# Pooled attention and a maxout feed-forward layer on one core: two shared score and AV buffers, an overlapped last token chunk, and a gate on the second batch's loads

## The chip, the cores and the metric

The kernel runs on one core of one Trainium2 chip. The metric is device time in microseconds (us) of one execution; lower is better. The core has TensorE (PE, with its weight loads as PEld), VectorE (DVE), ScalarE (ACT), GpSimd (POOL) and SyncE (SP), each working through its own list of instructions in order, and 16 DMA engines that all queues share.

## What is computed

Inputs are q, k, v of shape (8 batches, 8 heads, 576 tokens, 64) in float32, three weights w1, w2, w3 (512 x 768) and w_out (768 x 512). Keys and values are averaged over groups of 8 tokens, so that each head has 72 pooled keys. The result is (4608, 512) in float32.

```python
k_p = k.reshape(B, H, Sp, pool, D).mean(axis=3)
v_p = v.reshape(B, H, Sp, pool, D).mean(axis=3)
scores = scale * np.matmul(q, k_p.transpose(0, 1, 3, 2))
attn = softmax(scores)                     # over the 72 pooled keys
attn_out = np.matmul(attn, v_p)
x = attn_out.transpose(0, 2, 1, 3).reshape(B * S, H * D)
h = np.maximum(np.maximum(x @ w1, x @ w2), x @ w3)
out = h @ w_out
```

## The kernel before

The work is staged by batch. `load` (L56) issues three loads of a batch: `kt` and `vt` (1.18 MB each) from SP's queue, and `qb` from POOL's queue, which turns float32 into bfloat16 on the way. Two buffers of each exist (pool `ld`). After the loads of batch 0, POOL builds two identity matrices and issues the loads of the three weights `mw` and of `mwo` on its queue (L79, L80).

`prep` (L93) folds the 8 tokens of each group by adding halves: three steps on `kt` into `kp2`, twice written (L98, L101), on DVE for batch 0 and on POOL for the others; and three steps on `vt` into `vp_all`, always on POOL. TensorE transposes `qb` in three groups of six into `pqt` (L114), ACT copies each group to `qT` (L116). TensorE transposes `kp2` into `pkt` (L120), and DVE spreads it into `kz` (L124), whose zeros let one matmul take even or odd tokens.

`heads` (L129) makes, for each of 8 heads, two matmuls into `psc` (L135) and one exponential on ACT, `et` (L138). `psc` takes two PSUM banks, and there is one `psc` buffer. `values` (L145) goes over the batch's 576 tokens in five chunks: four of 128 and one of 64, the short one last in even batches and first in odd ones. For each chunk it makes 8 matmuls into `pav` (L151; one buffer of two banks), a reciprocal and a product on DVE (`rcp` L157, `xn` L159), four transposes into `pxt` (L164) and a copy on ACT into `xT` (L168). `pqt`, `pkt` and `pxt` share a single bank, tag `tr`.

`moe` (L171) takes 512 tokens: 72 matmuls of 512 columns into `pw` (L179, three banks), the maxima on ACT and DVE (L184, L187, L190), then 24 matmuls into `po` (L196), a copy on ACT (`osb`, L200) and the stores of the output from SP (L204). There are nine such blocks; block n is emitted after `values(n+1)`, and the last two after batch 7.

The order on each engine is not the written order: a scheduler places the instructions of all stages, so that `moe(n)` is mixed with `prep`, `heads` and `values` of batch n+1. Each engine then takes its list strictly in order, and a buffer is given out again when its last reader has finished.

Of the kernel before, what the change touches and what calls it, by code (L numbers as in the profile page):

```python
# [10 lines left out]
ALU = mybir.AluOpType  # L11
# [3 lines left out]
def kernel(  # L15
# [11 lines left out]
    nc = tc.nc  # L27
    dt = mybir.dt
    F32, BF16, F16 = dt.float32, dt.bfloat16, dt.float16

    B, H, S, D = q.shape
    POOL = 8
    Sp = S // POOL
# [19 lines left out]
    etp = ctx.enter_context(tc.tile_pool(name="etp", bufs=16))  # L53
    psp = ctx.enter_context(tc.tile_pool(name="psp", bufs=1, space=PSUM))

    def load(b):  # L56
        kt = ld.tile([96, 6, POOL, D], F32, name="kt", tag="kt")
        nc.sync.dma_start(out=kt, in_=k[b].rearrange(  # L58
            "h s d -> (h s d)").rearrange("(p i j d) -> p i j d", p=96, i=6, j=POOL))
        vt = ld.tile([Sp, H, POOL, D], F32, name="vt", tag="vt")  # L60
        nc.sync.dma_start(out=vt, in_=v[b].rearrange(
            "h (sp j) d -> sp h j d", j=POOL))
        qb = ld.tile([128, 2, NT, D], BF16, name="qb", tag="qb")
        nc.gpsimd.dma_start(out=qb, in_=q[b].rearrange(  # L64
            "h s d -> (h s d)").rearrange("(g p t d) -> p g t d", g=2, p=128, t=NT))
        return kt, vt, qb

    first = load(0)

    ident = const.tile([128, 128], BF16, name="ident", tag="ident")  # L70
    make_identity(nc, ident)
    identh = const.tile([128, 128], F16, name="identh", tag="identh")
    make_identity(nc, identh)

    w_sb = [const.tile([128, KCH, DFF], F16, name=f"mw{wi}", tag=f"mw{wi}")
            for wi in range(3)]
    wo_sb = const.tile([128, JCH, C], F16, name="mwo", tag="mwo")
    for t, wap in zip(w_sb, (moe_w1, moe_w2, moe_w3)):
        nc.gpsimd.dma_start(out=t, in_=wap.rearrange("(kc p) j -> p kc j", p=128))  # L79
    nc.gpsimd.dma_start(out=wo_sb,  # L80
                        in_=moe_w_out.rearrange("(jc p) c -> p jc c", p=128))

    vp_all = const.tile([Sp, B, H, 65], F16, name="vp", tag="vp")
# [7 lines left out]
    xT = const.tile([128, KCH, TOK], F16, name="xT", tag="xT")  # L91

    def prep(b, kt, vt, qb):  # L93
        eng = nc.vector if b == 0 else nc.gpsimd
        kp2 = sb2.tile([96, 6, 2, D], BF16, name="kp2", tag="kp2")
        def fold(e, t, outs):
            for n in (4, 2):
                e.tensor_tensor(out=t[:, :, 0:n, :], in0=t[:, :, 0:n, :],  # L98
                                in1=t[:, :, n:2 * n, :], op=ALU.add)
            for o in outs:  # L100
                e.tensor_tensor(out=o, in0=t[:, :, 0, :], in1=t[:, :, 1, :],  # L101
                                op=ALU.add)

        fold(eng, kt, [kp2[:, :, 0, :], kp2[:, :, 1, :]])
        fold(nc.gpsimd, vt, [vp_all[:, b, :, 0:D]])

        qT = sb2.tile([128, 2, NI, 128], BF16, name="qT", tag="qT")
        qTf = qT.rearrange("p g i c -> p (g i) c")
        for m in range(3):
            pqt = psp.tile([128, 6, 128], BF16, name="pqt", tag="tr", bufs=1)  # L110
            for u in range(6):
                n = 6 * m + u
                g, i = n // NI, n % NI
                nc.tensor.transpose(pqt[:, u, :], qb[:, g, 2 * i:2 * i + 2, :],  # L114
                                    ident)
            nc.scalar.copy(out=qTf[:, 6 * m:6 * m + 6, :], in_=pqt)  # L116

        pkt = psp.tile([128, 6, 96], BF16, name="pkt", tag="tr", bufs=1)
        for i in range(6):
            nc.tensor.transpose(pkt[:, i, :], kp2[:, i, :, :], ident[0:96, 0:96])  # L120
        kz = kz_all[b % 2]
        for par in range(2):
            rows = slice(64 * par, 64 * par + 64)
            nc.vector.tensor_copy(  # L124
                out=kz[rows, par].rearrange("p h (r i) -> p h r i", i=6),
                in_=pkt[rows].rearrange("p i (h r) -> p h r i", h=H))
        return qT, kz

    def heads(b, qT, kz):  # L129
        ets = []  # L130
        for h in range(H):
            psc = psp.tile([Sp, 2, 512], F32, name="psc", tag="psc", bufs=1)
            mov = qT[:, h // 4, :, 32 * (h % 4):32 * (h % 4) + 32]
            for par in range(2):
                nc.tensor.matmul(psc[:, par, 0:288], kz[:, par, h, :], mov,  # L135
                                 start=True, stop=True)
            et = etp.tile([Sp, S], F16, name="et", tag="et")
            nc.scalar.activation(  # L138
                out=et.rearrange("p (i a r) -> p i a r", a=2, r=NR),
                in_=psc[:, :, 0:288].rearrange("p a (i r) -> p i a r", r=NR),  # L140
                func=FT.Exp, scale=1.0 / 64.0)
            ets.append(et)
        return ets

    def values(b, ets):  # L145
        c0 = 0
        for n in ((128, 128, 128, 128, 64) if b % 2 == 0
                  else (64, 128, 128, 128, 128)):
            pav = psp.tile([128, 2, 512], F32, name="pav", tag="pav", bufs=1)
            for h in range(H):  # L150
                nc.tensor.matmul(  # L151
                    pav[0:n, h // 4, 65 * (h % 4):65 * (h % 4) + 65],
                    ets[h][:, c0:c0 + n], vp_all[:, b, h, :],
                    start=True, stop=True)
            pv = pav[0:n, :, 0:260].rearrange("p g (h e) -> p g h e", e=65)
            rcp = sb3.tile([128, 2, 4], F32, name="rcp", tag="rcp")
            nc.vector.reciprocal(out=rcp[0:n], in_=pv[:, :, :, 64])  # L157
            xn = sb3.tile([128, 2, 4, D], F16, name="xn", tag="xn")
            nc.vector.tensor_tensor(  # L159
                out=xn[0:n], in0=pv[:, :, :, 0:D],  # L160
                in1=rcp[0:n].to_broadcast([n, 2, 4, D]), op=ALU.mult)
            pxt = psp.tile([128, KCH, 128], F16, name="pxt", tag="tr", bufs=1)
            for kc in range(KCH):
                nc.tensor.transpose(  # L164
                    pxt[:, kc, 0:n], xn[0:n, kc // 2, 2 * (kc % 2):2 * (kc % 2) + 2, :],
                    identh[0:n, 0:n])
            g0 = S * b + c0
            nc.scalar.copy(out=xT[:, :, g0:g0 + n], in_=pxt[:, :, 0:n])  # L168
            c0 += n

    def moe(n):  # L171
        col = slice(NB * n, NB * n + NB)
# [32 lines left out]

    done = 0
    for b in range(B):
        loaded = first if b == 0 else load(b)
        qT, kz = prep(b, *loaded)
        ets = heads(b, qT, kz)  # L210
        values(b, ets)
        while b >= 1 and (done + 1) * NB <= b * S:
            moe(done)
            done += 1
# [33 lines left out]
```

## Time and profile before

| | us |
|---|---|
| median of 3 runs | 305.67 |
| lowest and highest | 305.3 and 309.04 |
| the profiled execution, device time | 308.39 |
| its span, first to last instruction | 306.6 |
| its busy time on PE, ACT, DVE, POOL | 257.3, 133.0, 127.8, 124.6 |

The span is what the rows of the trace describe; 1.8 us of the profiled execution lie outside it. A row's first number is its start in us from the beginning of the span, where the view is one in order of time.

### The profile page before, as it was taken

To read this page: it belongs to the slowest core of one execution; us is meant where nothing else is said; L and a number is where in the kernel's file an instruction comes from. 1 tells how busy PE (TensorE), PEld (TensorE's weight loads), DVE (VectorE), ACT (ScalarE), POOL (GpSimd) and SP (SyncE) were. 2 spreads that over 40 slices of the span, in tenths; PEclk is the share of its full clock that TensorE was granted. 3 is DMA by queue.
4 is the path that set the end of the run, shared out by engine and by line. 5 is a ranking of instruction groups with operands and counts; after the bars stand their busy time and mean duration, and the time that the engine had idled before them with its cause. 6 is when DMAs were issued, how large, how long until landed. Compare 5 with 4: busy or idle time off the path is not lost.

```text
span 306.6 us, 4320 instructions
## 1 busy us (share of the span) xinstructions
PE 257.3 (84%) x1664; PEld 130.4 (43%) x1664; DVE 127.8 (42%) x211; ACT 133.0 (43%) x219; POOL 124.6 (41%) x72
## 2 busy tenths in 40 slices
PE   0144470299999999999999999999999999999991
PEld 0022330154455555445555544555554445444440
DVE  6410330043626563354537254625645262551530
ACT  1034220135476545545674654466546636214221
POOL 6059799749999997969600030000000000000000
PEclk9999996579999999999999999999999999999998
DMA  7999999988644986982610450050022003104014
GB/s 175 264 268 252 229 237 211 234 186 202 158 103 104 216 198 151 246 183 67 118 38 0 112 104 3 9 131 1 0 70 69 2 0 94 45 0 121 19 25 114
DMA packets 17078, 36.47 MB, mean 119 GB/s; under 512 B 2720, under 2 KB 5024, under 8 KB 16288
## 3 DMA queue, kind: packets, MB, share of 16 engines
q1 hardware_dynamic: 12512, 28.32, 35.7%
q0 software_dynamic: 4544, 7.87, 14.8%
q8 instruction: 13, 0.21, 0.3%
q14 instruction: 9, 0.07, 0.1%
HBM read 34.60 MB, written 9.44 MB: 144 GB/s over the span
## 4 chain that ended last, share of the span: by engine, by line
PE 78%; DMA 18%; POOL 1%; DVE 0%; ACT 0%; issue 0%; SPq 0%; ACTq 0%
PE pw L179 46%; PE po L196 15%; DMA qb<-in_q_dram 12%; DMA vt<-in_v_dram 6%; PE psc L135 5%; PE pav L151 4%; PE pqt L114 3%; PE pxt L164 3%; POOL vt L98 1%; PE pkt L120 1%; DVE t L187 0%; DVE xn L159 0%; ACT xT L168 0%; ACT osb L200 0%; SPq L58 0%
## 5 line engine op out<-in xcount | busy, mean ns | idle before, releaser
L179 PE MATMUL pw<-xT,mw 128*128 128x512 f16 x648 | 162.0, 386 | 0.1
L179 PEld LDWEIGHTS <-mw 128*128 128x128 f16 x648 | 57.8, 99 | 53.9 <-issue 2.5
L187 DVE TENSOR_TENSOR t<-t,pw 128x512 f16<-128x512 f16 x54 | 37.0, 686 | 88.9 <-PE pw L179 77.7
L98 POOL TENSOR_TENSOR vt<-vt 72x2048 f32<-72x2048 f32 (+1 forms) x16 | 54.8, 3425 | 16.1 <-DMA vt<-in_v_dram 15.6
L138 ACT ACTIVATE et<-psc 72x576 f16<-72x576 f32 x64 | 41.4, 646 | 34.1 <-PE psc L135 34.1
L196 PE MATMUL po<-mwo,hT 128*128 128x512 f16 x216 | 51.7, 379 | 0.0
L190 DVE TENSOR_TENSOR hT<-t,pw 128x512 f16<-128x512 f16 x54 | 37.0, 685 | 29.9 <-PE pw L179 28.5
L184 ACT CAST t<-pw 128x512 f16<-128x512 f32 x54 | 31.6, 585 | 41.1 <-PE pw L179 40.4
L114 PE MATMUL pqt<-ident,qb 128*128 128x128 bf16 x144 | 13.9, 241 | 30.6 <-DMA qb<-in_q_dram 28.7
L98 POOL TENSOR_TENSOR kt<-kt 96x1536 f32<-96x1536 f32 (+1 forms) x14 | 36.6, 2614 | 3.1 <-DMA kt<-in_k_dram 2.7
L116 ACT COPY qT<-pqt 128x768 bf16<-128x768 bf16 x24 | 19.3, 802 | 41.9 <-PE pqt L114 41.7
L168 ACT COPY xT<-pxt 128x512 f16<-128x512 f16 (+1 forms) x40 | 21.7, 543 | 33.3 <-PE pxt L164 33.1
L135 PE MATMUL psc<-qT,kz 128*72 128x288 bf16 x128 | 29.5, 304 | 6.3 <-ACT et L138 5.1
L196 PEld LDWEIGHTS <-hT 128*128 128x128 f16 x216 | 19.6, 98 | 20.6 <-DVE hT L190 0.4
L200 ACT COPY osb<-po 128x512 f32<-128x512 f32 x36 | 21.1, 587 | 16.7 <-PE po L196 15.1
L159 DVE TENSOR_TENSOR xn<-pav,rcp 128x512 f16<-128x512 f32 (+1 forms) x40 | 27.5, 687 | 1.0
L114 PEld LDWEIGHTS <-qb 128*128 128x128 bf16 x144 | 11.4, 109 | 38.3 <-DMA qb<-in_q_dram 29.5
L151 PE MATMUL pav<-vp,et 72*128 72x65 f16 (+1 forms) x320 | 27.0, 203 | 0.4 <-ACT et L138 0.4
L135 PEld LDWEIGHTS <-kz 128*72 128x72 bf16 x128 | 14.9, 118 | 25.0 <-issue 7.2
L157 DVE RECIPROCAL rcp<-pav 128x8 f32<-128x8 f32 (+1 forms) x40 | 8.2, 205 | 35.5 <-PE pav L151 35.5
L151 PEld LDWEIGHTS <-et 72*128 72x128 f16 (+1 forms) x320 | 18.2, 105 | 10.5 <-issue 6.4
L64 POOL DMA_DIRECT2D qb<-in_q_dram x8 | 6.0, 752 | 33.7 <-PE pqt L114 32.9
(22 smaller groups left out, 82.9 us busy)
## 6 DMA issues: line engine op xcount, KB each, us to landing
kt<-in_k_dram SPq DMA_DIRECT2D x8, 1152.0 KB, 12.4
vt<-in_v_dram SPq DMA_DIRECT2D x8, 1152.0 KB
out_dram<-osb SPq DMA_DIRECT2D x144, 64.0 KB, 1.7
qb<-in_q_dram POOLq DMA_DIRECT2D x8, 576.0 KB, 8.6
mw<-in_moe_w_dram POOLq DMA_DIRECT2D x3, 768.0 KB, 27.5
mwo<-in_moe_w_out_dram POOLq DMA_DIRECT2D x1, 768.0 KB, 50.8
```

Of the source, the lines that this page charges most:

```text
L98: e.tensor_tensor(out=t[:, :, 0:n, :], in0=t[:, :, 0:n, :], in1=t[:, :, n:2 * n, :], op=ALU.add)
L114: nc.tensor.transpose(pqt[:, u, :], qb[:, g, 2 * i:2 * i + 2, :], ident)
L135: nc.tensor.matmul(psc[:, par, 0:288], kz[:, par, h, :], mov, start=True, stop=True)
L138: nc.scalar.activation(out=et.rearrange("p (i a r) -> p i a r", a=2, r=NR), in_=psc[:, :, 0:288].rearrange("p a (i r) -> p i a r", r=NR), ...
L151: nc.tensor.matmul(pav[0:n, h // 4, 65 * (h % 4):65 * (h % 4) + 65], ets[h][:, c0:c0 + n], vp_all[:, b, h, :], start=True, stop=True)
L159: nc.vector.tensor_tensor(out=xn[0:n], in0=pv[:, :, :, 0:D], in1=rcp[0:n].to_broadcast([n, 2, 4, D]), op=ALU.mult)
L168: nc.scalar.copy(out=xT[:, :, g0:g0 + n], in_=pxt[:, :, 0:n])
L179: nc.tensor.matmul(pw, w_sb[wi][:, kc, bass.ts(jc, 128)], xT[:, kc, col], start=(kc == 0), stop=(kc == KCH - 1))
L184: nc.scalar.copy(out=t, in_=pw)
L187: nc.vector.tensor_tensor(out=t1, in0=t, in1=pw, op=ALU.max)
L190: nc.vector.tensor_tensor(out=hT[:, jc, :], in0=t, in1=pw, op=ALU.max)
L196: nc.tensor.matmul(po, hT[:, jc, bass.ts(mm, 128)], wo_sb[:, jc, :], start=(jc == 0), stop=(jc == JCH - 1))
```

## The change

- `psc` and `pav` come from one ring of two buffers (tag `att`, `bufs=2`) in place of one buffer each. The PSUM use stays four banks.
- The last chunk of every batch is the 128 tokens from 448 on; its first 64 tokens are computed a second time and not copied (`keep`). No chunk of 64 is left.
- The loads of `kt` and `vt` of all batches from the second on wait for the third weight (`w_dma[2]`). `kt` of batch 0 is loaded in two halves.
- The fold of `kt` for batches 0 and 1 is done on DVE in two halves; batch 1's was on POOL.
- The second of the three `qT` copies of batch 0 goes from ACT to DVE.

```diff
-    def load(b):
+    def load(b, after=None):
...
+        if b == 0:
+            loads = [nc.sync.dma_start(out=kt[:, i:i + 3], in_=ksrc[:, i:i + 3])
+                     for i in (0, 3)]
+        else:
+            loads = [nc.sync.dma_start(out=kt, in_=ksrc)]
+        loads.append(nc.sync.dma_start(out=vt, in_=vsrc))
...
+        if after is not None:
+            for x in loads:
+                tc.add_manual_dep(x.ins, after.ins.name, mybir.DependencyInfo(
+                    mybir.DependencyClass.Sync, mybir.DependencyReason.DATA),
+                    reason="weights first")
...
-        fold(eng, kt, [kp2[:, :, 0, :], kp2[:, :, 1, :]])
+        if b < 2:
+            for i in (slice(0, 3), slice(3, 6)):
+                fold(nc.vector, kt[:, i], [kp2[:, i, 0, :], kp2[:, i, 1, :]])
+        else:
+            fold(nc.gpsimd, kt, [kp2[:, :, 0, :], kp2[:, :, 1, :]])
...
-            nc.scalar.copy(out=qTf[:, 6 * m:6 * m + 6, :], in_=pqt)
+            if b == 0 and m == 1:
+                nc.vector.tensor_copy(out=qTf[:, 6 * m:6 * m + 6, :], in_=pqt)
+            else:
+                nc.scalar.copy(out=qTf[:, 6 * m:6 * m + 6, :], in_=pqt)
...
-            psc = psp.tile([Sp, 2, 512], F32, name="psc", tag="psc", bufs=1)
+            psc = psp.tile([Sp, 2, 512], F32, name="psc", tag="att", bufs=2)
...
-        c0 = 0
-        for n in ((128, 128, 128, 128, 64) if b % 2 == 0
-                  else (64, 128, 128, 128, 128)):
-            pav = psp.tile([128, 2, 512], F32, name="pav", tag="pav", bufs=1)
+        for c0, keep in ((0, 0), (128, 0), (256, 0), (384, 0), (448, 64)):
+            pav = psp.tile([128, 2, 512], F32, name="pav", tag="att", bufs=2)
...
-            nc.scalar.copy(out=xT[:, :, g0:g0 + n], in_=pxt[:, :, 0:n])
-            c0 += n
+            nc.scalar.copy(out=xT[:, :, g0 + keep:g0 + 128],
+                           in_=pxt[:, :, keep:128])
...
-        loaded = first if b == 0 else load(b)
+        loaded = first if b == 0 else load(b, w_dma[2])
```

On SP, the list begins with the loads. Before, the first six rows of it are these, the loads of batches 0, 1 and 2; DMAHW and DMASW in a wait are the semaphores of loads from SP's and from POOL's queue.

```order
L243 UNCONDITIONAL_BRANCH [waits barrier_Pool_Activation_PE_DVE_SP_release]
L58 DMA kt<-in_k_dram 96x3072
L61 DMA vt<-in_v_dram 72x8x512
L58 DMA kt<-in_k_dram 96x3072
L61 DMA vt<-in_v_dram 72x8x512
L58 DMA kt<-in_k_dram 96x3072 [waits DMAHW0_49,DVE_49]
```

In the changed kernel the same place on SP reads as follows.

```order
L258 UNCONDITIONAL_BRANCH [waits barrier_Pool_Activation_PE_DVE_SP_release]
L63 DMA kt<-in_k_dram 96x1536 x2
L67 DMA vt<-in_v_dram 72x8x512
L66 DMA kt<-in_k_dram 96x3072 [waits DMASW3_49]
L67 DMA vt<-in_v_dram 72x8x512
L66 DMA kt<-in_k_dram 96x3072 [waits DMAHW1_49,DMAHW0_49,DVE_49]
```

The second `kt` load now stands behind a wait on the fourth load of POOL's queue, which is the third weight, and the loads behind it on SP stand with it.

On DVE, before, the fold of batch 0 is followed by `kz` and at once by the first chunk of `values(0)`.

```order
L98 TENSOR_TENSOR kt<-kt 96x6x256 [waits DMAHW0_49]
L98 TENSOR_TENSOR kt<-kt 96x6x128 [waits DVE_49]
L101 TENSOR_TENSOR kp_104<-kt 96x6x64 [waits DVE_49]
L101 TENSOR_TENSOR kp_104<-kt 96x6x64
L124 COPY kz_99<-pkt 64x576 [waits PE_49]
L124 COPY kz_99<-pkt 64x576
L157 RECIPROCAL rcp<-pav 128x8 [waits PE_49]
L159 TENSOR_TENSOR xn<-pav,rcp 128x512 [waits DVE_49]
```

In the changed kernel DVE's list at the same place is this; kz_100 is batch 0's, and the rows with DMAHW3 and kp_292 belong to batch 1.

```order
L131 COPY qT<-pqt 128x768 [waits PE_49]
L141 COPY kz_100<-pkt 64x576 [waits PE_49]
L141 COPY kz_100<-pkt 64x576
L108 TENSOR_TENSOR kt<-kt 96x3x256 [waits DMAHW3_49]
L108 TENSOR_TENSOR kt<-kt 96x3x256
L172 RECIPROCAL rcp<-pav 128x8 [waits PE_49] x2
L174 TENSOR_TENSOR xn<-pav,rcp 128x512 [waits DVE_49] x2
L108 TENSOR_TENSOR kt<-kt 96x3x128 x2
L172 RECIPROCAL rcp<-pav 128x8 [waits PE_49]
L172 RECIPROCAL rcp<-pav 128x8 [waits DVE_49,PE_49]
L174 TENSOR_TENSOR xn<-pav,rcp 128x512 [waits DVE_49] x2
L111 TENSOR_TENSOR kp_292<-kt 96x3x64
```

Batch 1's fold, which waits for its `kt` load, has come to stand ahead of the first reciprocal of batch 0.

On ACT, before, a middle batch (4) has its eight exponentials in groups of two and three between the copies of `moe`.

```order
L184 CAST t_1558<-pw_1553 128x512 [waits DVE_49,PE_49]
L138 ACTIVATE et<-psc 72x576 [waits PE_49] x2
L184 CAST t_1578<-pw_1573 128x512 [waits DVE_49,PE_49]
L138 ACTIVATE et<-psc 72x576 [waits PE_49] x3
L184 CAST t_1598<-pw_1593 128x512 [waits DVE_49,PE_49]
L138 ACTIVATE et<-psc 72x576 [waits PE_49] x3
L184 CAST t_1618<-pw_1613 128x512 [waits DVE_49,PE_49]
```

In the changed kernel a middle batch (5) has them in two groups of four.

```order
L199 CAST t_1923<-pw_1918 128x512 [waits DVE_49,PE_49]
L155 ACTIVATE et<-psc 72x576 [waits PE_49] x4
L199 CAST t_1943<-pw_1938 128x512 [waits DVE_49,PE_49]
L155 ACTIVATE et<-psc 72x576 [waits PE_49] x4
L199 CAST t_1963<-pw_1958 128x512 [waits DVE_49,PE_49]
```

The exponentials of a batch stand closer together: 13 `pw` matmuls lie on TensorE between the second half of a batch's first `psc` and the `pav` behind its last one, where there were four between each two heads.

## Rows read from the trace of the kernel before

**Rows 1.** The page: shares of the chain that ended last, by engine.
```profile
PE 78%; DMA 18%; POOL 1%; DVE 0%; ACT 0%; issue 0%; SPq 0%; ACTq 0%
```

**Rows 2.** The chain in order of time: start, duration (us), what.
```profile
1.18 17.71 DMA vt<-in_v_dram
18.97 4.44 POOL vt L98
23.41 36.13 DMA qb<-in_q_dram
...
258.73 15.54 PE pw L179 x72
```

**Rows 3.** Timeline, the start: start, duration (us), instructions, [idle before <- releaser].
```profile
22.16 0.65 ACT L138 ACTIVATE et<-psc 72x576 f16<-72x576 f32 x1 [2.82 <-PE psc L135]
...
23.53 0.65 ACT L138 ACTIVATE et<-psc 72x576 f16<-72x576 f32 x1 [0.73 <-PE psc L135]
...
41.25 1.87 PE L179 MATMUL pw<-xT,mw 128*128 128x512 f16 x4
...
59.59 0.82 PE L114 MATMUL pqt<-ident,qb 128*128 128x128 bf16 x6 [14.40 <-DMA qb<-in_q_dram]
```

**Rows 4.** Stretches from one batch's first transpose to the next's: busy us, clock, DMA.
```profile
60.00:89.45 29.45, 29.45 (x189) 14.81 (x188) 13.19 (x23) 14.65 (x24) 23.63 (x12) 0.91 0.73 169
89.45:116.76 27.31, 27.26 (x199) 14.41 (x197) 13.83 (x24) 15.76 (x26) 26.27 (x13) 1.00 0.74 168
116.76:145.40 28.64, 28.59 (x200) 14.55 (x197) 13.87 (x24) 15.62 (x26) 23.35 (x11) 1.00 0.69 161
145.40:172.72 27.32, 27.27 (x199) 14.42 (x197) 13.83 (x24) 15.76 (x26) 5.22 (x5) 1.00 0.28 57
172.72:202.12 29.40, 29.05 (x199) 14.36 (x197) 13.87 (x24) 15.64 (x26) 2.68 (x3) 1.00 0.29 61
202.12:229.68 27.56, 27.51 (x199) 14.39 (x197) 13.86 (x24) 15.64 (x26) 0.00 (x0) 1.00 0.16 40
229.68:258.73 29.05, 29.00 (x197) 14.29 (x195) 13.86 (x24) 15.64 (x26) 0.00 (x0) 1.00 0.14 36
```

**Rows 5.** Loads: the weights' issues and landings, POOL's queue (packets, MB, share).
```profile
2.96 2.27 POOL L79 DMA_DIRECT2D mw<-in_moe_w_dram x3
...
DMA to landing us min/median/max: 21.6/27.5/37.4
...
q0 software_dynamic: 4544, 7.87, 14.8%
```

**Rows 6.** Two `kt` loads, issued at 104.46 and at 41.17 us; last number: us to landing.
```profile
kt<-in_k_dram SPq DMA_DIRECT2D x1, 1152.0 KB, 8.1
...
kt<-in_k_dram SPq DMA_DIRECT2D x1, 1152.0 KB, 15.1
```

**Rows 7.** Groups by line and shape, DVE: busy us, mean ns of one, idle before.
```profile
L98 DVE TENSOR_TENSOR kt<-kt 96x768 f32<-96x768 f32 x1 | 1.0, 954 | 0.0
L159 DVE TENSOR_TENSOR xn<-pav,rcp 128x512 f16<-128x512 f32 x32 | 22.0, 689 | 0.8
L157 DVE RECIPROCAL rcp<-pav 128x8 f32<-128x8 f32 x32 | 6.6, 207 | 27.8 <-PE pav L151 27.8
```

**Rows 8.** Timeline of PE, two heads of batch 4, then two of batch 5.
```profile
152.54 0.41 PE L135 MATMUL psc<-qT,kz 128*72 128x288 bf16 x2
152.78 0.19 PE L151 MATMUL pav<-vp,et 72*128 72x65 f16 x1
...
153.68 0.41 PE L135 MATMUL psc<-qT,kz 128*72 128x288 bf16 x2
...
180.10 0.41 PE L135 MATMUL psc<-qT,kz 128*72 128x288 bf16 x2
180.44 0.22 PE L151 MATMUL pav<-vp,et 72*64 72x65 f16 x1
...
181.46 0.41 PE L135 MATMUL psc<-qT,kz 128*72 128x288 bf16 x2
```

More of the change, by code (lines that the diff above doesn't have):

```diff
@@ L54 @@
     psp = ctx.enter_context(tc.tile_pool(name="psp", bufs=1, space=PSUM))
-    def load(b):
+    def load(b, after=None):
         kt = ld.tile([96, 6, POOL, D], F32, name="kt", tag="kt")
-        nc.sync.dma_start(out=kt, in_=k[b].rearrange(
-            "h s d -> (h s d)").rearrange("(p i j d) -> p i j d", p=96, i=6, j=POOL))
+        ksrc = k[b].rearrange("h s d -> (h s d)").rearrange(
+            "(p i j d) -> p i j d", p=96, i=6, j=POOL)
         vt = ld.tile([Sp, H, POOL, D], F32, name="vt", tag="vt")
-        nc.sync.dma_start(out=vt, in_=v[b].rearrange(
-            "h (sp j) d -> sp h j d", j=POOL))
+        vsrc = v[b].rearrange("h (sp j) d -> sp h j d", j=POOL)
+        if b == 0:
[4 more added lines that the diff above has]
+        loads.append(nc.sync.dma_start(out=vt, in_=vsrc))
         qb = ld.tile([128, 2, NT, D], BF16, name="qb", tag="qb")
@@ L77 @@
     wo_sb = const.tile([128, JCH, C], F16, name="mwo", tag="mwo")
-    for t, wap in zip(w_sb, (moe_w1, moe_w2, moe_w3)):
-        nc.gpsimd.dma_start(out=t, in_=wap.rearrange("(kc p) j -> p kc j", p=128))
+    w_dma = [nc.gpsimd.dma_start(out=t,
+                                 in_=wap.rearrange("(kc p) j -> p kc j", p=128))
+             for t, wap in zip(w_sb, (moe_w1, moe_w2, moe_w3))]
     nc.gpsimd.dma_start(out=wo_sb,
@@ L93, in prep @@
     def prep(b, kt, vt, qb):
-        eng = nc.vector if b == 0 else nc.gpsimd
         kp2 = sb2.tile([96, 6, 2, D], BF16, name="kp2", tag="kp2")
@@ L145, in values @@
     def values(b, ets):
-        c0 = 0
-        for n in ((128, 128, 128, 128, 64) if b % 2 == 0
-                  else (64, 128, 128, 128, 128)):
-            pav = psp.tile([128, 2, 512], F32, name="pav", tag="pav", bufs=1)
+        for c0, keep in ((0, 0), (128, 0), (256, 0), (384, 0), (448, 64)):
+            pav = psp.tile([128, 2, 512], F32, name="pav", tag="att", bufs=2)
             for h in range(H):
                 nc.tensor.matmul(
-                    pav[0:n, h // 4, 65 * (h % 4):65 * (h % 4) + 65],
-                    ets[h][:, c0:c0 + n], vp_all[:, b, h, :],
+                    pav[:, h // 4, 65 * (h % 4):65 * (h % 4) + 65],
+                    ets[h][:, c0:c0 + 128], vp_all[:, b, h, :],
                     start=True, stop=True)
-            pv = pav[0:n, :, 0:260].rearrange("p g (h e) -> p g h e", e=65)
+            pv = pav[:, :, 0:260].rearrange("p g (h e) -> p g h e", e=65)
             rcp = sb3.tile([128, 2, 4], F32, name="rcp", tag="rcp")
-            nc.vector.reciprocal(out=rcp[0:n], in_=pv[:, :, :, 64])
+            nc.vector.reciprocal(out=rcp, in_=pv[:, :, :, 64])
             xn = sb3.tile([128, 2, 4, D], F16, name="xn", tag="xn")
             nc.vector.tensor_tensor(
-                out=xn[0:n], in0=pv[:, :, :, 0:D],
-                in1=rcp[0:n].to_broadcast([n, 2, 4, D]), op=ALU.mult)
+                out=xn, in0=pv[:, :, :, 0:D],
+                in1=rcp.to_broadcast([128, 2, 4, D]), op=ALU.mult)
             pxt = psp.tile([128, KCH, 128], F16, name="pxt", tag="tr", bufs=1)
@@ L164, in values @@
                 nc.tensor.transpose(
-                    pxt[:, kc, 0:n], xn[0:n, kc // 2, 2 * (kc % 2):2 * (kc % 2) + 2, :],
-                    identh[0:n, 0:n])
+                    pxt[:, kc, :],
+                    xn[:, kc // 2, 2 * (kc % 2):2 * (kc % 2) + 2, :], identh)
             g0 = S * b + c0
-            nc.scalar.copy(out=xT[:, :, g0:g0 + n], in_=pxt[:, :, 0:n])
-            c0 += n
+            nc.scalar.copy(out=xT[:, :, g0 + keep:g0 + 128],
+                           in_=pxt[:, :, keep:128])
     def moe(n):
```

## Prediction

> **What bounds the kernel now.** I read the chain that ended last first. TensorE holds 78% of it and DMA 18% [rows 1], so the time has two parts. In order of time [rows 2], the first 59.6 us are loads: the `vt` load of batch 0, POOL's first fold of it, and then, issued behind that fold at 23.41, the `qb` load of batch 1, which takes 36 us. From there to the end the chain is TensorE. The timeline of the start shows the join [rows 3]: TensorE begins `moe(0)` at 41.25, makes eight `pw` matmuls, and then stands 14.40 us at the transposes of batch 1's `qb` until 59.59. The stretches by batch [rows 4] show the second part: from 60 us on TensorE is busy all the time, 27.3 to 27.6 us in even batches (2, 4, 6) and 28.6 to 29.4 in odd ones (3, 5, 7). The last two blocks of `moe` begin at 258.73 [rows 2] and are not touched. So the change is worth what it takes from the start of batch 1, and from each of seven stretches.
>
> **The gate, and when batch 1's keys come.** Before, the SP loads of batches 1 and 2 run beside the weights. The third weight lands at 41.9: the last of three issues in the 2.27 us from 2.96 on, 0.76 apart, begins at 4.5, and 37.4 pass to its landing [rows 5]. In the changed kernel nothing from SP's queue moves between the `vt` load's end at 18.9 [rows 2] and that landing. The first weight landed at 2.96 + 21.6 = 24.6, so at 18.9 between two and three weights are still to come; I take 2.5. POOL's queue needs 14.8% of 306.6 us, or 45.4 us, for 7.87 MB [rows 5], which is 5.8 us a MB when the engines serve it alone, 4.5 us a weight of 0.786 MB, and 11.3 us for 2.5. The gate opens at 18.9 + 11.3 = 30.2, and the `kt` load goes out some 0.4 later, at 30.6. Bounds: two weights give 28, no speed-up at all 41.9.
>
> From issue to landing a `kt` load takes 8.1 us with an empty queue ahead and 15.1 with a `vt` load ahead [rows 6]. SP's queue is empty when the gate opens, so I take 8.1: batch 1's keys are there at 38.7.
>
> On one point the notes differ from this. The Trainium skill, "DMA: Bandwidth & Descriptors", section "Anatomy of one DMA", gives a transfer about 2.0 us plus its bytes at 436 GB/s, an estimate of 4.7 us for `kt`. The row with an empty queue shows 8.1. With 4.7 in place of 8.1 the sum below would be 3.4 us lower.
>
> **What waits behind it on DVE.** DVE takes its list in order, and batch 1's fold stands ahead of batch 0's first reciprocal. TensorE has batch 0's first `pav` long before: two `psc` buffers let an exponential start every 0.65 to 0.7 us instead of every 1.37 (22.16 to 23.53, rows 3), which ends `heads(0)` some 5 us earlier, but DVE stands until 38.7 all the same. So this gain, the half loads of `kt` and the `qT` copy moved to DVE (0.7 us by `xn`, of 512 elements, to 1.1 by size) are covered by that wait; without it the copy would cost about its time once. Then DVE does, by [rows 7]: two folds at 0.95; two reciprocals at 0.21 and two products at 0.69; two folds of half that size at 0.48; the next two reciprocals and products; and of the rest two `kp` pieces (a quarter, 0.24 each), a reciprocal and a product. That is 1.9 + 1.8 + 0.96 + 1.8 + 1.38 = 7.8 us. One bank for all transposes makes the fourth chunk wait once for a copy on ACT, an estimate of 1.2 for four transposes (six take 0.82, rows 3) and a copy of some 0.6 (the exponential's 0.65 for 576 elements, rows 3, brought to 512). Behind the last product come four transposes (0.6) and three of the first `pw` matmuls at the low clock (1.87 / 4 = 0.47 each, rows 3, 1.3 in all). TensorE reaches the transposes of batch 1 at 38.7 + 7.8 + 1.2 + 1.9 = 49.6 us, against 59.59.
>
> **Is `qb` there by then?** Its issue stands at the same place on POOL, behind the same fold, and behind the weights in POOL's queue. At 30.2 the fourth weight and `qb` are ahead, 0.786 + 0.59 MB, 7.9 us alone. Shared with batch 1's SP loads it is at most doubled: 38 to 46. It is there, with 3.6 us to spare. `vt` of batch 1 lands some 10 us behind `kt`, near 49 (a load of the same bytes), and its fold on POOL takes about 8 (4.44 for the first step, rows 2, then a half and a quarter), which is 57. The first `pav` of batch 1 has 33 `pw`, 8 pairs of `psc` and 24 transposes ahead of it on TensorE, some 11 us at the full clock and more at the low one, so that it comes past 60.
>
> Four `pw` matmuls fewer are done at that point than before (4 x 0.216 = 0.9 us; 0.216 is 15.54 / 72, rows 2). The start gives 59.6 - 49.6 - 0.9 = 9.1 us. Its bounds: `kt` landing at 36 gives 12, at 50.4 a loss of 2.6.
>
> **The seven stretches.** Odd batches cost more where one `pav` matmul of the 64-token chunk stands between heads. In batch 4 the distance from head to head is 1.14 us, in batch 5 1.36, with the same four `pw` between [rows 8]: the 72*64 form costs 0.2 us each time that TensorE goes into it and out, seven times in a batch, 1.5 us. That is most of what odd stretches have over even ones. Mean of the even ones: 27.40; batches 3, 5 and 7 together 87.09, which is 4.9 over three even ones [rows 4]. Batch 1's stretch holds the slow clock as well (0.91), so I give it the same 1.6. Without the 64-row forms all seven are like even ones: 6.5 us. The 64 tokens computed twice cost four transposes of 64 more columns a batch, 0.1 us, which the even batches regain by losing their own 64-row chunk.
>
> What can eat this is ACT. The exponentials now stand in groups of four, and two buffers shared with `pav` let TensorE run only two heads ahead. In that part ACT has 8 exponentials at 0.69 and 3 copies at 0.6, 7.3 us, TensorE 8 pairs of `psc` at 0.24 [rows 8] and 13 `pw` at 0.216, 4.8. If nothing overlapped, TensorE would stand 2.5 us in each stretch; if DVE and ACT keep up as they do now, none. I take the even level, the nearest row of this work without a 64-token chunk between heads, with bounds of -0.5 and +2.5 a stretch.
>
> **Sum.** 9.1 + 6.5 = 15.6 us. The profiled execution would go from 308.39 to 292.8. It lies 2.7 above the median of the runs, so against 305.67 I predict 290.
>
> **Rivals.**
> - *The loads follow the notes' figure.* Then `kt` lands 3.4 us sooner, and the weights, as bytes, about 2 sooner: 290 - 5.5 = 284.5. Against it stand the 8.1 us and the 5.8 us a MB of the rows.
> - *The gate opens no earlier* (41.9), because POOL's queue goes no faster alone. `kt` lands at 42.3 + 8.1 = 50.4, TensorE reaches batch 1 at 61.3, the start loses 2.6, and 305.67 + 2.6 - 6.5 = 301.8. For it: low DMA rates are to be seen wherever one queue runs alone. Against it: 45.4 us for the whole queue. The same page's section "Rules for kernel authors" asks for a load to be issued early and waited for late; batch 1's `kt` and `vt` are made to do the opposite.
> - *ACT takes over in the heads.* 2.5 us a stretch, 17.5 in seven: 290 + 17.5 = 307.5. For it: the sums of busy time above. Against it: both buffers are full when the groups begin, and before nothing showed TensorE waiting for ACT in the stretches.
> - *Slower: the gated `kt` load is late for DVE.* With the gate at 41.9 and the load in the crowd (15.1), it lands at 57.4, TensorE reaches batch 1 at 68.3, the start loses 9.6, and 305.67 + 9.6 - 6.5 = 308.8. The point from which the change loses is a landing past 54.3 us, where the start costs the 6.5 that the stretches give.
>
> **How the numbers follow.** The forecast has 0.77, with 284 to 296 of its own; the notes' figure 0.06; the late gate 0.06; ACT 0.07; the late load 0.04. About 2% can be told from no change here, which is 299.6 to 311.8. Faster by more than that: nearly all of the forecast and the first rival, 0.83. Slower by more: what is left of the last two when they come together, 0.04. Within: 0.13. The range, 283.5 to 300, takes the bounds of the `kt` landing and of the stretches and leaves out the last three.
>
> **What would show it.** In the new profile: batch 1's `kt` lands near 39 and DVE's first fold of it begins then; the first `rcp` comes after it, near 40; the transposes of batch 1 begin near 50 with no idle for `qb`; the stretches of batches 2 to 7 are alike, near 27.4; TensorE idles little between heads. Wrong would be: the gate past 35, TensorE still waiting for `qb`, or TensorE idle for `et` in the stretches, more than 1 us in each.

## The result and the profile after

The changed kernel takes 289.93 us (median of 4 runs, 288.4 to 290.31), the kernel before 306.72 beside it (median of 4, 305.3 to 309.04). The ratio is 0.9436, with a 95% interval of 0.9362 to 0.9511. The profiled execution took 289.99 us with a span of 288.2; the profiled execution of the kernel before took 308.39, with a span of 306.6. The spans differ by 18.4 us. One run of one later kernel, over 1.5% above the fastest of the same kernel, lies in a slower state and is left out of its median.

The chain that ended last, first its shares by engine, from the page of the changed kernel (before: [rows 1]):

```profile
PE 77%; DMA 14%; ACT 2%; DVE 1%; issue 1%; POOL 1%; SPq 0%; ACTq 0%; POOLq 0%
```

The same chain in order of time: start, duration in us, what.

```profile
4.47 21.32 DMA mw<-in_moe_w_dram
25.81 9.92 DMA kt<-in_k_dram
35.75 1.82 DVE kt L108 x2
...
72.12 10.18 DMA out_dram<-osb
...
239.83 15.54 PE pw L194 x72
```

In [rows 2] the start of the chain was `vt`, POOL's fold, and a `qb` load of 36 us. Now it is the third weight, the `kt` load of batch 1 that waited for it, and DVE's fold of that load. A store of the output stands in the chain for the first time, at 72 us. The last two blocks of `moe` begin at 239.83 where they began at 258.73.

The timeline of the start: start, duration, engine and line, what, number of instructions, [idle before <- releaser].

```profile
25.81 0.32 SPq L66 DMA_DIRECT2D kt<-in_k_dram  x1
...
35.75 1.82 DVE L108 TENSOR_TENSOR kt<-kt 96x768 f32<-96x768 f32 x2 [16.66 <-DMA kt<-in_k_dram]
37.60 0.28 DVE L172 RECIPROCAL rcp<-pav 128x8 f32<-128x8 f32 x2
...
38.59 0.61 PE L179 MATMUL pxt<-identh,xn 128*128 128x128 f16 x4 [9.96 <-DVE xn L174]
39.05 1.01 DVE L108 TENSOR_TENSOR kt<-kt 96x384 f32<-96x384 f32 x2
...
45.34 6.93 POOL L108 TENSOR_TENSOR vt<-vt 72x2048 f32<-72x2048 f32 x2 [17.79 <-DMA vt<-in_v_dram]
46.05 0.85 PE L128 MATMUL pqt<-ident,qb 128*128 128x128 bf16 x6
...
48.48 0.50 PE L128 MATMUL pqt<-ident,qb 128*128 128x128 bf16 x6
...
82.40 0.59 ACT L215 COPY osb<-po 128x512 f32<-128x512 f32 x1 [0.74 <-DMA out_dram<-osb]
```

The gate opens at 25.81, `kt` lands at 35.73, and DVE, which has stood 16.66 us for it, folds it ahead of the first reciprocal. TensorE stands 9.96 us for DVE's first product, and begins the transposes of batch 1 at 46.05, with no idle for `qb`. Before, that row stood at 59.59 behind 14.40 us of idle [rows 3].

The stretches from one batch's first transpose to the next's, in the same columns as [rows 4]: busy us of PE, PEld, DVE, ACT and POOL, the granted clock, DMA share, GB/s.

```profile
46.05:73.89 27.84, 27.73 (x193) 14.81 (x192) 13.57 (x24) 14.63 (x25) 27.35 (x13) 1.00 0.89 217
73.89:102.22 28.33, 27.61 (x198) 14.66 (x197) 13.51 (x24) 15.19 (x26) 27.84 (x15) 1.00 0.75 178
102.22:129.90 27.68, 27.63 (x198) 14.53 (x196) 13.49 (x24) 15.20 (x26) 27.19 (x13) 1.00 0.82 193
129.90:157.21 27.31, 27.22 (x198) 14.67 (x197) 13.54 (x24) 15.15 (x26) 17.19 (x9) 1.00 0.47 105
157.21:184.69 27.48, 27.37 (x197) 14.69 (x196) 13.54 (x24) 15.12 (x26) 2.68 (x3) 1.00 0.29 61
184.69:212.17 27.48, 27.37 (x197) 14.68 (x196) 13.53 (x24) 15.12 (x26) 0.00 (x0) 1.00 0.16 39
212.17:239.83 27.66, 27.55 (x198) 14.78 (x197) 13.54 (x24) 15.12 (x26) 0.00 (x0) 1.00 0.15 39
```

Batches 3, 5 and 7 were at 28.6 to 29.4 and are now at 27.5 to 27.7. Batch 2 alone became longer, 28.33 for 27.31, and TensorE is idle there for 0.72 us (28.33 less 27.61).

From these rows the 18.4 us divide as follows. At the start of batch 1 TensorE is 13.54 us earlier (59.59 - 46.05), with four `pw` fewer done (0.86): 12.7. Batches 3, 5 and 7 give 4.27 (87.09 to 82.82). Batch 1 gives 2.88 (29.86 counted from 59.59, against 27.84, and the four `pw` that are done in it now). Batches 2, 4 and 6 lose 0.93 (82.19 to 83.12). The last two blocks, to the end of the span, take 48.37 for 47.87, a loss of 0.5. Together 12.7 + 4.3 + 2.9 - 0.9 - 0.5 = 18.4. The starts in [rows 4] from 89.45 on, and the 239.83 here, lie some 0.17 us behind those of the timeline; no term moves by more than that.

### The profile page after: what moved, and what is told of

Same layout as the page of the kernel before. It is cut to its first block, busy times and chain, and to the rows that moved or that the text cites. A ratio compares the mean times of both kernels' runs of the same rounds, so it can differ in the third digit from the quotient of the medians.

```text
span 288.2 us, 4331 instructions
## 1 busy us (share of the span) xinstructions
PE 248.6 (86%) x1664; PEld 131.2 (46%) x1664; DVE 129.3 (45%) x224; ACT 128.0 (44%) x218; POOL 117.4 (41%) x68
## 4 chain that ended last, share of the span: by engine, by line
PE 77%; DMA 14%; ACT 2%; DVE 1%; issue 1%; POOL 1%; SPq 0%; ACTq 0%; POOLq 0%
PE pw L194 47%; PE po L211 15%; DMA mw<-in_moe_w_dram 7%; PE psc L152 6%; PE pxt L179 4%; DMA out_dram<-osb 4%; DMA kt<-in_k_dram 3%; PE pav L166 3%; PE pqt L128 3%; ACT xT L183 2%; PE pkt L137 1%; DVE kt L108 1%; POOL mw L88 1%; ACT osb L215 0%; DVE xn L174 0%
## 5 line engine op out<-in xcount | busy, mean ns | idle before, releaser
L194 PE MATMUL pw<-xT,mw 128*128 128x512 f16 x648 | 163.8, 382 | 0.7 <-ACT xT L183 0.7
L194 PEld LDWEIGHTS <-mw 128*128 128x128 f16 x648 | 60.4, 98 | 51.0 <-issue 1.1
L211 PE MATMUL po<-mwo,hT 128*128 128x512 f16 x216 | 48.1, 379 | 0.0
L155 ACT ACTIVATE et<-psc 72x576 f16<-72x576 f32 x64 | 37.4, 645 | 11.4 <-PE psc L152 11.3
L108 POOL TENSOR_TENSOR kt<-kt 96x1536 f32<-96x1536 f32 (+1 forms) x12 | 31.4, 2617 | 0.4
L133 ACT COPY qT<-pqt 128x768 bf16<-128x768 bf16 x23 | 18.4, 801 | 24.0 <-PE pqt L128 23.7
L174 DVE TENSOR_TENSOR xn<-pav,rcp 128x512 f16<-128x512 f32 x40 | 26.7, 684 | 0.4
L179 PE MATMUL pxt<-identh,xn 128*128 128x128 f16 x160 | 16.5, 229 | 11.4 <-DVE xn L174 10.8
L179 PEld LDWEIGHTS <-xn 128*128 128x128 f16 x160 | 11.9, 102 | 21.9 <-DVE xn L174 17.4
L166 PE MATMUL pav<-vp,et 72*128 72x65 f16 x320 | 18.8, 200 | 3.3 <-POOL vp L111 3.3
L128 PEld LDWEIGHTS <-qb 128*128 128x128 bf16 x144 | 10.9, 105 | 20.5 <-DMA qb<-in_q_dram 12.0
L166 PEld LDWEIGHTS <-et 72*128 72x128 f16 x320 | 15.6, 103 | 7.3 <-ACT et L155 3.2
## 6 DMA issues: line engine op xcount, KB each, us to landing
mw<-in_moe_w_dram POOLq DMA_DIRECT2D x3, 768.0 KB, 18.3
```

The lines of the kernel that those rows point to most:

```text
L108: e.tensor_tensor(out=t[:, :, 0:n, :], in0=t[:, :, 0:n, :], in1=t[:, :, n:2 * n, :], op=ALU.add)
L155: nc.scalar.activation(out=et.rearrange("p (i a r) -> p i a r", a=2, r=NR), in_=psc[:, :, 0:288].rearrange("p a (i r) -> p i a r", r=NR), ...
L166: nc.tensor.matmul(pav[:, h // 4, 65 * (h % 4):65 * (h % 4) + 65], ets[h][:, c0:c0 + 128], vp_all[:, b, h, :], start=True, stop=True)
L179: nc.tensor.transpose(pxt[:, kc, :], xn[:, kc // 2, 2 * (kc % 2):2 * (kc % 2) + 2, :], identh)
L194: nc.tensor.matmul(pw, w_sb[wi][:, kc, bass.ts(jc, 128)], xT[:, kc, col], start=(kc == 0), stop=(kc == KCH - 1))
L211: nc.tensor.matmul(po, hT[:, jc, bass.ts(mm, 128)], wo_sb[:, jc, :], start=(jc == 0), stop=(jc == JCH - 1))
```

## The experiments

The theory was the prediction's: the gate gives the start, the 128-token last chunk gives the stretches, the rest is covered. The rivals: the ring of two buffers gives the stretches; the move of batch 1's fold to DVE gives the start; the loads come as early without the gate. Each time is a median beside runs of the kernel before on the same chip.

**The change without the gate.**

```diff
-        loaded = first if b == 0 else load(b, w_dma[2])
+        loaded = first if b == 0 else load(b)
```

> The changed kernel without the wait on the third weight; batch 1's fold stays on DVE ahead of the first reciprocal. Theory (the gate gives the start): batch 1's keys land near 25 again, but its qb lands near 59 as before, TensorE reaches batch 1's transposes near 59 in place of 46, and the time is 290 + 13 = 303 us. Rival (the start comes from the order and the moved fold, the gate is beside the point): qb lands before 45, time within 2 us of 290.

Measured: 301.91 us against 307.56, ratio 0.9831 (0.9784 to 0.9877), near the 303 of the theory. The gate is worth 12 us (301.91 less 289.93). The timeline, the `qb` load's row (KB, us to landing), and POOL's queue from 20 to 30 us (packets, MB, share), show how:

```profile
57.79 0.82 PE L128 MATMUL pqt<-ident,qb 128*128 128x128 bf16 x6 [18.82 <-DMA qb<-in_q_dram]
...
qb<-in_q_dram POOLq DMA_DIRECT2D x1, 576.0 KB, 34.6
...
q0 software_dynamic: 867, 1.23, 68.2%
```

The same queue in the changed kernel, from 20 to 27 us:

```profile
q0 software_dynamic: 1088, 1.38, 116.9%
```

And the changed kernel's `qb` load:

```profile
qb<-in_q_dram POOLq DMA_DIRECT2D x1, 576.0 KB, 15.4
```

Without the gate, POOL's queue writes 1.23 MB in 10 us, beside SP's loads (0.82 MB of it from 20 to 27); with it, 1.38 MB in 7 us, in which SP's queue moves nothing. The `qb` load, which is behind the weights in that queue, takes 34.6 us without the gate and 15.4 with it. Without the gate TensorE stands 18.82 us for it, as it stood 14.40 in [rows 3]. What the gate brings forward is `qb`; `kt`, which it holds back, becomes the last to come.

**Batch 1's `kt` fold on POOL.**

```diff
-        if b < 2:
+        if b < 1:
```

> The changed kernel with batch 1's kt fold on POOL again, where it stands ahead of the vt fold of batch 1, so that DVE goes from kz straight to batch 0's reciprocals. Theory (DVE's stand at 17.4 to 35.8 us costs the start): the first reciprocal comes near 29, moe(0) begins near 36, TensorE fills the time up to qb (38) and beyond, and the time falls by 5 to 9 us, to 281 to 285. Rival (POOL is then late): POOL folds kt from 35.7 to 43, vt from 45 to 53.5, TensorE stands at the first pav of batch 1 for vp, and the time stays within 2 us of 290.

Measured: 289.62 against 307.56, 0.9428 (0.9377 to 0.9479): as the change itself and as the rival had it, and 4.6 us or more above the theory's 281 to 285. DVE now makes the first reciprocal at 28.10, and TensorE reaches batch 1 at 38.55, 7.5 us earlier. The timeline and the first two stretches show where it went:

```profile
38.55 0.82 PE L128 MATMUL pqt<-ident,qb 128*128 128x128 bf16 x6 [2.53 <-DMA qb<-in_q_dram]
...
54.54 0.55 PE L166 MATMUL pav<-vp,et 72*128 72x65 f16 x7 [2.43 <-POOL vp L111]
...
75.67 0.58 ACT L215 COPY osb<-po 128x512 f32<-128x512 f32 x1 [1.88 <-DMA out_dram<-osb]
...
38.55:71.81 33.26, 30.76 (x194) 16.42 (x195) 13.52 (x24) 14.62 (x25) 29.32 (x16) 0.95 0.92 214
71.81:101.26 29.45, 27.53 (x197) 14.66 (x196) 13.53 (x24) 15.20 (x26) 28.88 (x15) 1.00 0.80 187
```

TensorE is earlier at batch 1, where it now stands 2.53 us for `qb`, and then waits for its folded values, which POOL has at 54.5; the first stretch takes 33.26 us for 27.84. Of these 5.42 us, 2.4 are idle time; for the rest TensorE is busy, 30.76 us for 27.73, at a granted clock of 0.95 over the stretch. In the second the copies on ACT wait for the stores, and it takes 29.45 for 28.33. The 6.5 us in these two eat nearly all of the gain. So DVE's wait for `kt` was not the last cause: behind it stand `qb` and `vt` of batch 1.

**The change with buffers of their own for `psc` and `pav`, one each.**

```diff
-psc = psp.tile([Sp, 2, 512], F32, name="psc", tag="att", bufs=2)
+psc = psp.tile([Sp, 2, 512], F32, name="psc", tag="psc", bufs=1)
...
-pav = psp.tile([128, 2, 512], F32, name="pav", tag="att", bufs=2)
+pav = psp.tile([128, 2, 512], F32, name="pav", tag="pav", bufs=1)
```

> The changed kernel with one psc and one pav buffer of their own, as before, in place of the shared ring of two. Theory (the ring gives next to nothing: heads(0) is covered by DVE's wait for kt, and in the stretches one buffer is enough): 290 us within 2, with stretches of 27.2 to 27.6. Rival (the ring carries the gain of the stretches): stretches of 28 us and more, time 294 or more.

Measured: 290.73 against 307.56, 0.9474 (0.9425 to 0.9522). Beside the overlapped chunk the ring gives nothing that can be told in the time: stretches 4 to 7 are 27.23 to 27.25 without it. In the trace it gives something at the start and takes it back in the stretches. Without it TensorE reaches batch 1 at 49.26 for 46.05 and batch 2 at 74.75 for 73.89, 0.86 us later; batches 3 to 6 then take 1.2 us less together (108.7 for 109.95). The theory had DVE's wait for `kt` cover all that the ring does in batch 0; it does not.

**The change with the chunks of before (one of 64).**

```diff
-        for c0, keep in ((0, 0), (128, 0), (256, 0), (384, 0), (448, 64)):
+        for n in ((128, 128, 128, 128, 64) if b % 2 == 0
+                  else (64, 128, 128, 128, 128)):
```

> The changed kernel with the chunks of before (a 64-token chunk, first in odd batches, last in even ones), ring and gate kept. Theory (the 64-row form costs 0.2 us at each switch): with the new order the chunk stands in one block and not between heads, so it costs two switches a chunk rather than seven: 0.3 us in each of eight batches at most, 290 to 293 us. Rival (the 64-row form as such costs what odd stretches had over even ones): odd stretches 1.6 us longer than even ones, 296 to 297 us.

Measured: 292.03 against 307.56, 0.95 (0.9455 to 0.9545). The stretch of batch 5, which was 29.40 in [rows 4], is here:

```profile
158.18:186.01 27.83, 27.78 (x197) 14.47 (x196) 13.43 (x24) 15.12 (x26) 2.69 (x3) 1.00 0.29 60
```

The theory's 290 to 293 held. Odd and even batches are alike (27.7 to 28.0 in batches 1 and 3 to 6), though odd ones have their chunk of 64 first. In this kernel's list of TensorE the 64-token matmuls stand in one block, not one between each two heads, and so the 1.5 us for going into the form and out seven times are gone here too. The overlap or the new order of the ring, either takes away most of the odd batches' excess; the gate does not, as the next kernel's batches 3 and 5 show (28.81 and 29.05).

**Before with the gate alone**, added to `load` as in the change; batch 1's fold stays on POOL.

> The kernel before with the gate alone: the kt and vt loads from batch 1 on wait for the third weight, nothing else is changed; batch 1's fold stays on POOL, so DVE does not stand for it. Theory (the gate alone makes qb early): qb of batch 1 lands near 38 in place of 59.5, TensorE reaches batch 1's transposes at 44 to 46, odd stretches stay near 29 and even ones near 27.4: before minus 12 to 14, 293 to 295 us. Rival (it needs the moved fold as well, POOL being too late with batch 1's kt and vt): the first stretch grows by over 5 us and the time is 299 or more.

Measured: 296.36 against 307.8, 0.9632 (0.9582 to 0.9683), 11.4 us. TensorE reaches batch 1 at 44.54. The first stretch takes 31.40; the timeline has a wait in it, and below it is its row:

```profile
55.11 0.19 PE L156 MATMUL pav<-vp,et 72*64 72x65 f16 x1 [2.22 <-POOL vp L106]
...
44.54:75.94 31.40, 29.15 (x190) 14.42 (x189) 13.87 (x24) 14.69 (x24) 28.59 (x13) 0.95 0.89 206
```

The theory had 293 to 295. The start is as it had it. The 1.4 to 3.4 us that are missing lie in the first two stretches. By the timeline's starts the first is 1.7 us longer than before (29.7), with the wait for batch 1's values; the second is 28.42 for 27.31, where a copy on ACT waits 1.53 us for the stores. Neither was in my sum.

**Before with the overlapped last chunk alone**, the loop of `values` as in the change.

> The kernel before with the overlapped last chunk alone. Theory (the 64-row form between heads costs 1.5 us in an odd batch): all stretches from batch 2 on come to 27.2 to 27.5, start as before, before minus 6, ratio 0.98. Rival (odd stretches are long for another reason, as their place among the stores or the loads): odd ones stay above 28.5, time within 2 us of before.

Measured: 300.33 against 307.8, 0.973 (0.9665 to 0.9794), 7.5 us.

**Before with the chunk of 64 last in every batch**, so that no 64-token matmul stands between heads, though each batch still has its short chunk.

```diff
-        for n in ((128, 128, 128, 128, 64) if b % 2 == 0
-                  else (64, 128, 128, 128, 128)):
+        for n in (128, 128, 128, 128, 64):
```

> The kernel before with the 64-token chunk last in every batch, nothing computed twice. Theory (what costs is the place of the 64-row form between the heads, not that it exists): stretches all near 27.4 as in the even batches of before, before minus 5.5, within 1.5 us of the overlapped form. Rival (the overlap itself is needed): odd stretches stay over 28.5.

Measured: 300.67 against 307.8, 0.9757 (0.9695 to 0.9819), 7.1 us: nearly all that the overlap gives. The stretch of batch 3, 28.64 in [rows 4], with the overlap alone:

```profile
114.89:141.89 27.00, 26.95 (x197) 14.48 (x196) 13.87 (x24) 15.83 (x26) 19.37 (x10) 1.00 0.79 182
```

and with the chunk of 64 moved to the end:

```profile
114.64:141.87 27.23, 27.18 (x198) 14.51 (x197) 13.88 (x24) 15.56 (x26) 22.44 (x11) 1.00 0.77 179
```

Batch 5, at 29.40 before, takes 27.26 with the overlap and 27.95 with the chunk moved. It was the place of the short chunk, not its size.

**Fold on POOL, own buffers, and eight `osb` buffers**, against the waits that the second experiment showed (its edit, the third's, and the line below).

```diff
-            osb = sb3.tile([128, C], F32, name="osb", tag="osb")
+            osb = sb3.tile([128, C], F32, name="osb", tag="osb", bufs=8)
```

> The changed kernel with batch 1's fold on POOL, one psc and one pav buffer of their own, and eight osb buffers in place of three. Theory (the 7.5 us that POOL's fold won at the start were given back by ACT's wait for stores behind the gated loads and by vp of batch 1): the second half of that is mended, the stretch of batch 2 falls from 29.5 to 27.5 and the later ones by 0.25 each, 285 to 287 us. Rival (vp of batch 1, bound by its vt load near 46, is all that counts): 288 to 290 us.

Measured: 286.22 (median of three runs) against 307.8, 0.929 (0.9215 to 0.9365), within the 285 to 287 of the theory. The same kernel ran again beside the next two:

> The kernel of the run before this one without the split, on the same chip for comparison: 285 to 288 us, TensorE standing some 4 us at batch 1's first pav and at half clock behind it.

Measured: 286.96 against 307.05, 0.9357 (0.9296 to 0.9417). The stretch of batch 2 is 27.12, for 29.45 in the second experiment. In its timeline and its windows of TensorE (busy us, granted clock, DMA share, GB/s), the values of batch 1 are late:

```profile
45.67 6.93 POOL L108 TENSOR_TENSOR vt<-vt 72x2048 f32<-72x2048 f32 x2 [2.69 <-DMA vt<-in_v_dram]
52.68 1.26 POOL L111 TENSOR_TENSOR vp<-vt 72x512 f16<-72x512 f32 x1
...
54.00 0.19 PE L166 MATMUL pav<-vp,et 72*128 72x65 f16 x1 [3.42 <-POOL vp L111]
...
50.00:55.00 5.00, 1.58 (x9) 1.00 0.84 193
55.00:60.00 5.00, 5.00 (x23) 0.66 0.71 172
```

TensorE stands 3.42 us, and in the 5 us behind that the granted clock is 0.66. The first stretch takes 30.72.

**The same, with batch 1's `vt` loaded and folded in two halves of four heads.**

```diff
+        if b == 1:
+            loads += [nc.sync.dma_start(out=vt[:, h:h + 4], in_=vsrc[:, h:h + 4])
+                      for h in (0, 4)]
...
-        fold(nc.gpsimd, vt, [vp_all[:, b, :, 0:D]])
+        for hs in (slice(0, 4), slice(4, 8)) if b == 1 else (slice(0, 8),):
+            fold(nc.gpsimd, vt[:, hs], [vp_all[:, b, hs, 0:D]])
```

> The last kernel (batch 1's kt fold on POOL, own buffers, eight osb) with batch 1's vt loaded and folded in two halves of four heads. Theory (vp of batch 1, a fold of 8.2 us behind a load that lands at 46.7, now sets the start): POOL folds the first half while the second is under way, vp is there near 51 in place of 54.9, TensorE does not stand at batch 1's first pav and its clock stays up, the first stretch falls by 4 to 7 us: 281 to 284 us. Rival (the stand only moves, to kz or to the loads of batch 2): 286 to 288 us.

Measured: 280.54 us (280.16 to 281.19) against 307.05, 0.914 (0.9082 to 0.9198), just under the 281 to 284 expected, and the best of all these kernels. Its timeline and windows at the same place:

```profile
43.01 3.69 POOL L112 TENSOR_TENSOR vt<-vt 72x1024 f32<-72x1024 f32 x2
46.77 0.72 POOL L115 TENSOR_TENSOR vp<-vt 72x256 f16<-72x256 f32 x1
...
49.46 0.19 PE L171 MATMUL pav<-vp,et 72*128 72x65 f16 x1
...
50.00:55.00 5.00, 5.00 (x32) 1.00 0.82 186
55.00:60.00 5.00, 5.00 (x39) 1.00 0.74 184
```

The first four heads' values are ready near 47.5 in place of 54, TensorE does not stand, and the clock stays at 1.00. The first stretch is 25.49 for 30.72: the 3.42 us of waiting, and some 1.7 of lower clock (5 us at 0.66). TensorE also reaches batch 1 0.96 us sooner (41.62 for 42.58).

**The change with own buffers and eight `osb` buffers.**

> The changed kernel with own psc and pav buffers and eight osb buffers, batch 1's fold left on DVE. Theory (ACT's wait for stores costs the second stretch 1.2 us, and nothing else changes): the stretch of batch 2 falls from 28.4 to 27.1, later ones stay at 27.1 to 27.3, 288 to 289.5 us. Rival (the stores' wait is hidden by other work): 290 to 291.

Measured: 289.09 against 307.05, 0.9411 (0.9363 to 0.9459). Batch 2's stretch is 27.11, where own buffers alone had 28.42, as expected: the wait of `osb` for its stores was worth 1.3 us in that stretch. The profiled executions of these two kernels differ by only 0.6 us (289.72 and 289.10), since TensorE reaches batch 1 0.84 us later here.

## Why the prediction was right, and where by luck

I predicted 290.0 us, faster; it is 289.93. The two large steps were right in kind, and the experiments bear both out: 11.4 us for the gate alone and 7.5 for the overlapped chunk alone. In the rows the start gave 12.7 for the 9.1 of the sum, past its bound of 12, and the stretches 6.2 for 6.5; the last two blocks, at nothing in the sum, lost 0.5. That the sum agrees to a tenth is luck. I had a gain of 15.6 and set it against the three runs' median of 305.67, 2.7 below the profiled execution that the sum was made on. The gain between profiled executions is 18.4, 2.8 more. These two errors cancel but for 0.1; the median itself is 306.72 with the fourth run.

- **The gate's opening, 30.2 predicted.** It opened at 25.8, below the bound of 28. Both factors of the term were too large. Two weights were still to come, not 2.5: with no load of batch 1 beside it the first landed at 18.3, where it had landed at 24.6, and batch 0's `vt` was there at 18.0. And a weight took 3.7 us, not the 4.5 that I had from the share of POOL's queue over the whole span, as the tile's landings say:

```profile
DMA to landing us min/median/max: 15.3/18.3/21.3
```

  With issues 0.76 apart these are landings at 18.3, 22.0 and 25.8. The share was the wrong measure, crowded or not. From 20 to 27 us, where POOL's queue has the engines to itself, it reads 116.9%, and 116.9% of 7 us for 1.38 MB are 5.9 us a MB, as over the whole span before (5.8). It adds up the times of packets that overlap, or it could not pass 100%. In elapsed time it is 7 us for 1.38 MB, 5.1 us a MB.
- **The `kt` load, 8.1 predicted.** It took 9.9 (25.81 to 35.73). The row I used was of a load at 104 us; here the fourth weight, `qb`, and the loads issued behind it (`vt` of batch 1, all three of batch 2) were under way beside it. The Trainium skill, "DMA: Bandwidth & Descriptors", section "Anatomy of one DMA", has its figure from DMAs of POOL's queue, and `kt` goes out on SP's; used for `kt`, as in the prediction, it is an estimate of 4.7 us. The trace has 9.9, but no row here shows a `kt` load with the engines to itself, so that neither number tests the figure. For the weights, which are on POOL's queue, its 436 GB/s gives an estimate of 3.6 us for 1.57 MB read, and the 3.7 between two landings in the trace agree.
- **From `kt`'s landing to TensorE at batch 1, 10.9 predicted** (7.8 + 1.2 + 1.9): 10.3. TensorE's time there comes out as 49.6 - 4.4 (gate) - 0.4 (the issue, which followed at once) + 1.8 (load) - 0.6 (list) = 46.0, and the row says 46.05.
- **`qb` in time, 38 to 46 predicted.** It landed at 37.9 (issued 22.46, 15.4 to landing). TensorE did not wait for it. `vt` of batch 1 landed at 45.3 for 49, and its values were ready at 53.6 for 57; both were covered, as predicted.
- **What DVE's wait covers.** I said that gains in batch 0's heads were covered by DVE's wait for `kt`. The wait did hold TensorE: taking it away brought batch 1 forward by 7.5 us. I did not see that this is worth nothing by itself, since batch 1's values come next. No run separates the half loads of `kt` and the `qT` copy on DVE (0.56 us).
- **The seven stretches, 6.5 predicted.** They gave 6.2 (4.27 + 2.88 - 0.93). Not all of it is the form: in batch 1 the overlap alone gave 1.8 (29.69 to 27.88 by the timeline's starts, at a granted clock of 0.90 in both), where the change gave 2.88. The cause, the 64-column form between heads, is shown by moving it to the end: 7.1 us with no overlap at all. But what I did not see is that the ring's new order alone would have done most of it. Batch 2's stretch has a wait that I had not counted, ACT for the stores: these stand behind a `kt` and a `vt` load in SP's queue (issued at 61.57 and 69.83).
- **The rivals.** ACT did not take over: the waits of TensorE hold this row, 1.5 us in all four times, where the rival needed 2.5 in each stretch.

```profile
PE psc L152 <- ACT et L155: 1.5, 4, 0.6
```

  The gate did open early, so the two rivals with a late gate fell. The Trainium skill's figure came nearer than I gave it credit for with the weights; `kt` came later than my own 8.1 and not sooner.
- **The last two blocks** took 0.5 us more than before. TensorE is busy 41.44 us there in both; from the start of the last copy to the end of the span pass 6.85 us for 6.35 (281.35 to 288.2, 300.25 to 306.6). So the 0.5 lies in the last stores; why they took longer stays open.

The parts do not quite add: 11.4 + 7.5 = 18.9 us alone, 16.8 together by the medians (17.4 by the change's ratio: 0.0564 times 307.8). The interval of each is some 2 us, so that this difference is not shown.

## What to carry to other kernels

When a load is gated to let others pass, ask which queue gets the time and what stands last once it has come: here the gate was worth 12 us, because `qb` sat behind the weights in the other queue, and the next things late were `kt`, then `vt`, in that order. A wait that covers a gain can be worth nothing to remove until the next one behind it goes as well; the fold on POOL gave 0, and with the half loads of `vt` and free buffers it was part of 9.4 us. Look where a short, odd-shaped piece of work stands before paying to remove it; moving it to the end of its batch gave 7.1 of 7.5 us.

## What the runs showed of the hardware

- **DVE's adds slow down beside POOL's.** With no gate, DVE folds batch 1's `kt` while POOL folds `vt`. The timeline of that kernel, and the row of the tile on DVE (ns min/median/max):

```profile
23.82 6.13 DVE L108 TENSOR_TENSOR kt<-kt 96x768 f32<-96x768 f32 x4 [3.30 <-DMA kt<-in_k_dram]
23.86 2.36 POOL L108 TENSOR_TENSOR vt<-vt 72x1024 f32<-72x1024 f32 x1
...
L108 DVE TENSOR_TENSOR kt<-kt x8: 543/720/3228, 6.3 to 29.4; 96x768 f32<-96x768 f32 x4, 96x384 f32<-96x384 f32 x4
```

  In the changed kernel, with POOL idle, the same four take 1.82 + 1.01 us (the rows at 35.75 and 39.05) and the longest single one 0.95. Here one takes 3.23, which is 2.28 more, close to the 2.36 of POOL's add beside it. The Trainium skill, "SBUF — State Buffer", section "SBUF: two separate sides", says that DVE and GpSimd share a pair of ports that one instruction holds to its end, for a DVE operation with two inputs in SBUF; this trace agrees.
- **The granted clock at the start.** The column reads 1.00 from 46.05 on, but six transposes there take 0.85 us and the same six 0.50 from 48.48 on. TensorE had stood 9.96 us until 38.59. In the kernel before, from 59.59 to 65.00, the column reads 0.50, and six transposes take 0.82 to 0.85 there. So the durations at 46.05 are those of the low level (1.2 GHz), where the column does not show it; nor does it for the 1.87 us of four `pw` in [rows 3] (1.00 from 41.25 to 45.20).
- **Stores behind loads.** A store of 64 KB lands in 1.7 us at the median and in 10.2 where it was issued (at 72 us) behind a `kt` and a `vt` load in SP's queue.
- **A copy out of PSUM on DVE** (128 x 768 into bfloat16) took 0.56 us, the same copy on ACT 0.80 in the mean. I had put it at 0.7 to 1.1.
